# First keys through two DMA queues, in halves of 64 partitions, and one load for the last heads' rows

## The chip, the cores and the metric

The kernel runs on one core of one Trainium2 chip. The core has a matrix engine (TensorE, PE in the profile), a vector engine (VectorE, DVE), a scalar engine (ScalarE, ACT), GpSimd (POOL) and SyncE (SP), which here only issues transfers. Transfers are issued from SP's queue and from ACT's queue. The metric is device time in microseconds: 193.44 us is the median of 3 runs before (193.33 to 193.98). The profiled execution took 193.34 us, and its span, on which all times below are counted, is 191.2 us.

## What is computed

One token is decoded with 32 heads over the last 4096 positions of a key and value cache, and the result is gated by a small multilayer network on the same input:

```python
xn = _layernorm(x)
q = (xn @ wq).reshape(1, 1, 32, 128)           # one query row for each head
k = k_cache[:, :, Sk - 4096:, :]               # 32 heads x 4096 x 128, bf16
v = v_cache[:, :, Sk - 4096:, :]
p = softmax((q @ k^T) * 128 ** -0.5)
s = (p @ v) @ wo                               # 4096 -> 512
g = silu(B(xn, w1, w2, w3, w4))                # layernorm, gelu, w3, gelu, w4
out = x + s * g
```

(The lines are shortened; B is the network.) With a sequence of one position every part of B's first layer is shifted out, so w1 has no effect on the output and the kernel doesn't load it. The keys and values are 32 MB each, 79 MB are moved in all, and each byte is used once.

## The kernel before

**Tiling.** The heads are handled in eight groups of four (G = 4). A group's keys are one tile `kv` of 128 partitions by 128 columns by 128 numbers in bf16, 4 MB; partition 4b + a holds block b of head a. `load_kv` (L95) loads such a tile as 128 rows, whole (32 KB a row) or cut along the columns. Group 0's keys come as two loads, columns 0 to 63 and 64 to 127 (L534), so that each has all 128 partitions.

**Scores.** Two engines share a group. VectorE takes the first 64 or 80 columns: `k_vector` (L312) multiplies a quarter of them with the query (product, L321) and sums it (L323), four pairs a group. TensorE takes the other columns: `k_turn` transposes them (L339), ScalarE copies the result out of PSUM (L342), and `k_scores` (L350) multiplies with the query. ScalarE separates the heads (`sm_own`, L359), VectorE adds them to the scores and finds the maximum (`sm_max`, L364, L366), and `sm_turn`, `sm_exp`, `sm_den` and `sm_rden` make the softmax a step later.

**Values and output.** `v_wide` (L427) multiplies a group's probabilities with its values, `v_turn`, `v_add` and `v_out` turn and scale the result. `ox_spread`, `ox_pick` and `y_wide` multiply heads 0 to 27 with wo. The last group's values come in three loads (columns 0 to 63, 64 to 95, 96 to 127). The last 32 columns go through `v_part` (L461), and the last four heads through `y_head`, which reads the tile `wo_rows`, loaded by `load_rows` (L414) as two loads of two heads.

**Order.** The loop at L531 runs ten steps. In step s the keys of group s are scored, and the values of group s - 2 are used. Inside the region opened at L527 the order of TensorE, VectorE and ScalarE is the order in which the code is written.

**Queues and buffers.** `load` (L75) issues every large load on SP, in program order: w2, w3, w4 (1280 KB), the remaining 96 rows of w4, the keys of groups 0, 1 and 2, and so on. ACT issues x twice and wq (4 MB). An issue that has to wait, for a free buffer or for an earlier landing, holds up those behind it on its queue. There are three key buffers: group 3's keys can be loaded only when VectorE and TensorE have finished with group 0's. There are two value buffers. The weights `wts` are freed before the first values are loaded, so that load waits for the last reader of the weights (the copy `hr`, L273, and the product after it).

Of the kernel before, what the change touches and what calls it, by code (L numbers as in the profile page):

```python
# [8 lines left out]
P = 128  # L9
BF16 = mybir.dt.bfloat16  # L10
# [8 lines left out]
G = 4  # L19
# [7 lines left out]
def kernel(  # L27
# [14 lines left out]
    nc = tc.nc  # L42
# [3 lines left out]
    _, H, Sk, Dh = A_k_cache.shape  # L46
# [3 lines left out]
    W0 = Sk - W  # L50
    assert W == 4096
    CP = G * W // P
    PB = P // G
# [6 lines left out]
    k_pool = ctx.enter_context(tc.tile_pool(name="k", bufs=K_BUFS))  # L60
# [11 lines left out]
    wts_guard = tc.tile_pool(name="wts", bufs=1)  # L72
    wts = wts_guard.__enter__()

    def load(dst, src):  # L75
        return tc.keep_in_program_order(nc.sync.dma_start(out=dst, in_=src))  # L76

    x_bf = small.tile([P, KC], BF16, name="x_bf")
    nc.scalar.dma_start(out=x_bf[:], in_=A_x.rearrange("a b (p c) -> p (a b c)", p=P))
# [3 lines left out]
    wq_sb = wts.tile([P, KC, HD], BF16, name="wq_sb")  # L83
    nc.scalar.dma_start(out=wq_sb[:].rearrange("p c n -> p (c n)"),
                        in_=A_wq.rearrange("(a b c) n -> b a (c n)", a=4, c=KC))
    w2_sb = wts.tile([P, KC, D], BF16, name="w2_sb")
    load(w2_sb[:], B_w2.rearrange("(p c) n -> p c n", p=P))
    w3_sb = wts.tile([P, KC, F], BF16, name="w3_sb")
# [1 line left out]
    w4_sb = wts.tile([P, 11, D], BF16, name="w4_sb")  # L90
    load(w4_sb[:, 0:10, :], B_w4[0:10 * P, :].rearrange("(p c) n -> p c n", p=P))
    load(w4_sb[0:96, 10, :], B_w4[10 * P:F, :])


    def load_kv(pool, cache, g, cuts=(0, CP)):  # L95
        t = pool.tile([P, CP, Dh], BF16, tag="kv", name="kv")
        src = cache[0, G * g:G * g + G, W0:, :].rearrange("a (b c) d -> b a (c d)", b=PB)
        dst = t[:].rearrange("p c d -> p (c d)")
        for c0, c1 in zip(cuts, cuts[1:]):
            load(dst[:, c0 * Dh:c1 * Dh], src[:, :, c0 * Dh:c1 * Dh])  # L100
        return t
# [115 lines left out]
    for b in range(2):  # L217
# [5 lines left out]
        for t in range(2):  # L223
            rows = slice(64 * t, 64 * t + 64)
            nc.scalar.copy(out=q_pair[rows, 4 * b:4 * b + 4, :, G * t:G * t + G].rearrange("p g l a -> p g a l"),
                           in_=qt_ps[rows].bitcast(BF16).rearrange("p g (a m l) -> p g a m l", a=G, l=2)[:, :, :, 0, :])
# [41 lines left out]
    for i, (col, w) in enumerate(terms):  # L268
        r = 32 * (i % 4)
# [41 lines left out]
    def k_open(g):  # L311
        st[g] = {  # L312
            "sT": ps_s.tile([P, CP - 64, G], FP32, tag="sT", name="sT"),
            "S": sm_pool.tile([P, CP], FP32, tag="S", name="S"),
        }

    def k_vector(g, kn, part):
        m = nd(g) // 4
        rows = slice(m * part, m * part + m)
        prod = prod_pool.tile([P, 20, Dh], BF16, tag="prod", name="prod")  # L320
        nc.vector.tensor_tensor(out=prod[:, 0:m, :], in0=kn[:, rows, :],  # L321
                                in1=q_bc[:, g:g + 1, :].to_broadcast([P, m, Dh]), op=ALU.mult)
        nc.vector.tensor_reduce(out=st[g]["S"][:, rows], in_=prod[:, 0:m, :], axis=AX.X, op=ALU.add)  # L323
# [3 lines left out]
    def batches(g):  # L327
        n, m = nd(g), CP - nd(g)
        k = -(-m // 8)
        edges = [n + 2 * (m // 2 * i // k) for i in range(k + 1)]  # L330
        return list(zip(edges, edges[1:]))

    def k_turn(g, kn, b):
        c0, c1 = batches(g)[b]
        n = (c1 - c0) // 2
        pt = ps_tr.tile([P, 4, P], FP32, tag="pt", name="pt")
        for i in range(n):
            c = c0 + 2 * i
            nc.tensor.transpose(pt[:, i, :], kn[:, c:c + 2, :].rearrange("p c d -> p (c d)").bitcast(FP32),  # L339
                                ident_f[:])  # L340
        kts[b] = kt_pool.tile([P, 4, 2 * P], BF16, tag="kt", name="kt")
        nc.scalar.copy(out=kts[b][:, 0:n, :], in_=pt[:, 0:n, :].bitcast(BF16))  # L342

    def k_scores(g, b):
        kt = kts.pop(b)
        c0, c1 = batches(g)[b]
        for i in range((c1 - c0) // 2):
            c = c0 + 2 * i - nd(g)
            for l in range(2):
                nc.tensor.matmul(st[g]["sT"][:, c:c + 2, :].rearrange("p c a -> p (c a)"),  # L350
                                 lhsT=kt[:, i, l::2], rhs=q_pair[:, g, l, :], start=(l == 0), stop=(l == 1))
# [44 lines left out]
    def sm_rden(g):  # L396
        s = st[g]
        s["rden"] = sm_pool.tile([P, G], FP32, tag="rden", name="rden")
        nc.vector.reciprocal(out=s["rden"][:], in_=s["den"][:])  # L399
# [7 lines left out]
    def load_wo(i):  # L407
        h0, n = blocks[i]
        load(wo_blk[i], A_wo[h0 * P:(h0 + n) * P, :].rearrange("(p t) n -> p t n", p=P))
# [4 lines left out]
    def load_rows(h, n):  # L414
        load(wo_rows[:, h - h_part:h - h_part + n, :],
             A_wo[h * P:(h + n) * P, :].rearrange("(h p) n -> p h n", p=P))
# [108 lines left out]
    NG = H // G  # L525
# [5 lines left out]
    for s in range(NG + LAG):  # L531
        h = s - LAG
        last = h == NG - 1
        kn = load_kv(k_pool, A_k_cache, s, (0, 64, CP) if s == 0 else (0, CP)) if s < NG else None  # L534
        if s == LAG:
            wts_guard.__exit__(None, None, None)
            v_pool = ctx.enter_context(tc.tile_pool(name="v", bufs=V_BUFS))
            wo_blk[2] = v_pool.tile([P, 4, D], BF16, tag="wo_4", bufs=1, name="wo_4")
            wo_rows = v_pool.tile([P, H - h_part, D], BF16, tag="wo_rows", bufs=1, name="wo_rows")
        if last:  # L540
            v = load_kv(v_pool, A_v_cache, h, cuts)
            for r in (H - G, H - 2):
                load_rows(r, 2)
        elif h >= 0:
            v = load_kv(v_pool, A_v_cache, h)
        if h == 3:
            wo_24 = k_pool.tile([P, 32, D], BF16, tag="kv", name="wo_24")
            wo_blk[0], wo_blk[1] = wo_24[:, 0:16, :], wo_24[:, 16:24, :]
            load_wo(0)
        if h == 5:  # L550
            load_wo(1)
            load_wo(2)

        if s < NG:
            nb = len(batches(s))

            def keys(b0, b1):
                for b in range(b0, b1):
                    k_turn(s, kn, b)
                    if b > 0:  # L560
                        k_scores(s, b - 1)

            k_open(s)
            k_vector(s, kn, 0)
            keys(0, 2)
            if s == 7:
                v_turn(h - 1)
                v_add(h - 1)
                v_out(h - 1)
            elif s > 1:  # L570
                sm_den(s - 2)
                sm_rden(s - 2)
            elif s == 1:
                sm_max(0)
            k_vector(s, kn, 1)
            keys(2, 4)
            if s == 7:
                sm_den(h)
                sm_rden(h)
                keys(4, nb - 2)  # L580
                sm_turn(s - 1)
                keys(nb - 2, nb)
            else:
                if s > 0:
                    sm_turn(s - 1)
                keys(4, nb)
            k_scores(s, nb - 1)
            sm_own(s)
            if s == 7:
                k_vector(s, kn, 2)  # L590
                v_wide(h, v)
                sm_exp(s - 1)
                v_turn(h)
                y_open()
                k_vector(s, kn, 3)
                v_add(h)
                v_out(h)
                ox_spread(1)
                sm_max(s)
                continue  # L600
            if s > 0:
                sm_exp(s - 1)
            if h > 0:
                v_turn(h - 1)
            k_vector(s, kn, 2)
            if h >= 0:
                v_wide(h, v)
            if h > 0:
                v_add(h - 1)
                v_out(h - 1)  # L610
            if s == 6:
                ox_spread(0)
            k_vector(s, kn, 3)
            if s == 6:
                ox_pick(0)
            if s > 0:
                sm_max(s)
        elif s == NG:
            ox_pick(1)
            sm_turn(NG - 1)  # L620
            sm_exp(NG - 1)
            y_wide(1, False)
            sm_den(NG - 2)
            sm_rden(NG - 2)
            y_wide(0, False)
            warm(3)
            v_wide(h, v)
            sm_den(NG - 1)
            sm_rden(NG - 1)
            v_turn(h)  # L630
            v_add(h)
            v_out(h)
            ox_spread(2)
        else:
            v_open(h)
            warm(3)
            v_wide(h, v, cuts[1], last=False)
            ox_pick(2)
            y_wide(2, True)
            nc.scalar.copy(out=y_sum[:], in_=yr[0][:].rearrange("p j n -> p (j n)"))  # L640
            v_wide(h, v, cuts[2], cuts[1])
            v_turn(h)
            v_add(h)
            rows_add(y_ps, ind, y_sum, False)
            v_part(h, v, cuts[2], CP)
            v_out(h)
            for r in range(H - G, H):
                y_head(r)
# [36 lines left out]
```

## Time and profile before

| What | Value |
|---|---|
| median time | 193.44 us |
| span of the profiled execution | 191.2 us |
| VectorE busy | 150.9 us (79%) |
| TensorE busy | 116.4 us (61%) |
| ScalarE busy | 89.2 us (47%) |
| moved by DMA | 79.02 MB, 413 GB/s over the span |
| wq landed | 17.6 us after its issue at 2.32 us |
| group 0's second half landed | 27.4 us after its issue at 4.71 us |
| group 1 of VectorE starts | 41.91 us |

How to read the profile: the second part of the page cuts the span into 40 slices of 4.8 us, and each digit is the busy share of an engine in tenths, 9 for 90% or more. A timeline line gives the start, the busy time, the engine, the line of the kernel, the operation with output and input, and in brackets how long the engine had been idle before it and what ended the wait. A line on a DMA issue gives the tile, the queue, the number of issues, the size of one and the median time from issue to landing. Buffer numbers are left out of names, so that w_sb is w2, w3 or w4.

### The profile page before, as it was taken

How to read it: one execution, taken by the hardware profiler on the slowest of the kernel's cores; microseconds unless marked ns; L12 is line 12 of the kernel's file. 1: busy time of each engine (PE TensorE's matmuls, PEld its weight loads, DVE VectorE, ACT ScalarE, POOL GpSimd, SP SyncE). 2: the span in 40 equal slices, each digit the busy share in tenths (PEclk: the TensorE clock that was granted, in tenths of full speed). 3: DMA queues.
4: the chain of work that ended last, by engine and by line, in shares of the span. 5: the costliest groups of instructions: out<-in, count | busy, mean ns of one | idle time of the engine just before them, and what ended most of it. 6: DMA issues, size and time to landing. Idle time of an engine off the chain costs nothing.

```text
span 191.2 us, 2839 instructions
## 1 busy us (share of the span) xinstructions
PE 116.4 (61%) x1159; PEld 74.2 (39%) x1159; DVE 150.9 (79%) x175; ACT 89.2 (47%) x191; POOL 2.3 (1%) x11
## 2 busy tenths in 40 slices
PE   1653754989825368256845772680888189739762
PEld 0430222767614334143334441540763077313322
DVE  1660159979999999999999999999999999980111
ACT  2001370888794076427464564542475148733120
POOL 2110000000000000000000000000000000000000
PEclk9999695555755557955695588557567858975998
DMA  6999999999999999999999999999999998999990
GB/s 211 447 430 404 431 418 439 439 439 437 432 434 439 432 429 432 432 439 432 422 432 432 418 422 418 452 439 435 439 432 434 435 432 372 471 425 405 420 371 32
DMA packets 4572, 79.02 MB, mean 413 GB/s; under 512 B 624, under 2 KB 1232, under 8 KB 1488
## 3 DMA queue, kind: packets, MB, share of 16 engines
q1 hardware_dynamic: 4264, 74.65, 91.6%
q10 hardware_dynamic: 296, 4.20, 5.1%
q8 instruction: 9, 0.15, 0.3%
q14 instruction: 3, 0.02, 0.0%
HBM read 78.84 MB, written 0.00 MB: 412 GB/s over the span
## 4 chain that ended last, share of the span: by engine, by line
DVE 46%; DMA 43%; PE 5%; ACT 3%; issue 1%; SPq 1%; ACTq 0%; DVEq 0%
DMA kv<-in_A_k_cache_dram 31%; DVE S L323 28%; DVE prod L321 15%; DMA kv<-in_A_v_cache_dram 10%; ACT kt L342 3%; DMA x_bf<-in_A_x_dram 2%; PE pt L339 2%; PE ov L427 1%; DVE m L366 1%; DVE S L364 1%; SPq L76 1%; PE sT L350 1%; DVE mx L374 1%; PE oT L461 1%; PE ot_ps L444 0%
## 5 line engine op out<-in xcount | busy, mean ns | idle before, releaser
L323 DVE TENSOR_REDUCE S<-prod 128x20 f32<-128x2560 bf16 (+1 forms) x32 | 86.0, 2686 | 1.1
L342 ACT COPY kt<-pt 128x1024 bf16<-128x1024 bf16 x52 | 51.2, 1013 | 40.4 <-PE pt L339 38.7
L339 PE MATMUL pt<-ident_f,kv 128*128 128x128 f32 x208 | 46.7, 376 | 10.8 <-DMA kv<-in_A_k_cache_dram 10.8
L321 DVE TENSOR_TENSOR prod<-kv,q_bc 128x2560 bf16<-128x2560 bf16 (+1 forms) x32 | 45.4, 1418 | 3.9 <-DMA kv<-in_A_k_cache_dram 3.7
L339 PEld LDWEIGHTS pt<-ident_f,kv 128*128 128x128 f32 x208 | 34.2, 196 | 14.4 <-DMA kv<-in_A_k_cache_dram 10.5
L350 PE MATMUL sT<-q_pair,kt 128*128 128x8 bf16 x416 | 19.4, 170 | 15.7 <-ACT kt L342 15.5
L350 PEld LDWEIGHTS <-kt 128*128 128x128 bf16 x416 | 16.4, 104 | 26.8 <-ACT kt L342 25.8
L427 PE MATMUL ov<-kv,pT 128*16 128x512 bf16 x248 | 22.0, 515 | 1.4 <-DMA kv<-in_A_v_cache_dram 1.4
L388 ACT ACTIVATE pT<-S,mb 128x128 bf16<-128x128 f32 x32 | 13.9, 573 | 0.3
L372 PE MATMUL mt_ps<-ident_f,m 128*1 128x128 f32 x8 | 2.9, 359 | 17.4 <-DVE rden L399 16.9
L433 ACT COPY ov_sb<-ov 128x512 f32<-128x512 f32 x8 | 4.7, 586 | 17.1 <-PE ov L427 17.1
L427 PEld LDWEIGHTS <-pT 128*16 128x16 bf16 x248 | 6.9, 109 | 13.2 <-issue 11.4
L359 ACT ACTIVATE own<-sT,par 128x48 f32<-128x48 f32 (+1 forms) x32 | 7.5, 356 | 3.7 <-PE sT L350 3.7
L444 PE MATMUL ot_ps<-ident_f,ov_sb 128*128 128x128 f32 x32 | 7.1, 359 | 2.9 <-ACT mb L384 1.9
L211 DVE CAST q_row<-qr_ps 128x512 bf16<-128x512 f32 x1 | 0.7, 692 | 9.9 <-PE qr_ps L208 9.9
L388 ACT ACTIVATION_READ_ACCUMULATOR pT<-S,mb 128x1 f32 x32 | 8.3, 258 | 0.0
L372 PEld LDWEIGHTS mt_ps<-ident_f,m 128*1 128x1 f32 x8 | 0.6, 80 | 17.9 <-DVE rden L399 17.2
L399 DVE RECIPROCAL rden<-den_ps 128x4 f32<-128x4 f32 x8 | 1.4, 175 | 7.0 <-PE den_ps L394 7.0
L381 PE MATMUL mb_ps<-md,par_t 5*128 5x4 f32 x16 | 3.9, 311 | 4.1 <-DVE md L376 4.1
L255 ACT ACTIVATE a_row<-a_ps 128x384 bf16<-128x384 f32 x1 | 0.5, 491 | 12.0 <-remote 12.0
L444 PEld LDWEIGHTS ot_ps<-ident_f,ov_sb 128*128 128x128 f32 x32 | 4.5, 178 | 3.9 <-ACT mb L384 2.3
L208 PE MATMUL qr_ps<-wq_sb,xq_bf 128*1 128x512 bf16 x32 | 3.1, 566 | 3.7 <-DMA wq_sb<-in_A_wq_dram 3.7
(122 smaller groups left out, 81.6 us busy)
## 6 DMA issues: line engine op xcount, KB each, us to landing
kv<-in_A_k_cache_dram SPq DMA_DIRECT2D x7, 4096.0 KB, 31.3
kv<-in_A_v_cache_dram SPq DMA_DIRECT2D x7, 4096.0 KB, 30.6
wq_sb<-in_A_wq_dram ACTq DMA_DIRECT2D x1, 4096.0 KB, 17.6
kv<-in_A_k_cache_dram SPq DMA_DIRECT2D x2, 2048.0 KB, 27.4
wo<-in_A_wo_dram SPq DMA_DIRECT2D x1, 2048.0 KB
kv<-in_A_v_cache_dram SPq DMA_DIRECT2D x1, 2048.0 KB
kv<-in_A_v_cache_dram SPq DMA_DIRECT2D x2, 1024.0 KB, 17.6
w_sb<-in_B_w_dram SPq DMA_DIRECT2D x1, 1376.0 KB, 9.1
```

What stands on the lines that cost most here:

```text
L321: nc.vector.tensor_tensor(out=prod[:, 0:m, :], in0=kn[:, rows, :], in1=q_bc[:, g:g + 1, :].to_broadcast([P, m, Dh]), op=ALU.mult)
L323: nc.vector.tensor_reduce(out=st[g]["S"][:, rows], in_=prod[:, 0:m, :], axis=AX.X, op=ALU.add)
L339: nc.tensor.transpose(pt[:, i, :], kn[:, c:c + 2, :].rearrange("p c d -> p (c d)").bitcast(FP32), ident_f[:])
L342: nc.scalar.copy(out=kts[b][:, 0:n, :], in_=pt[:, 0:n, :].bitcast(BF16))
L350: nc.tensor.matmul(st[g]["sT"][:, c:c + 2, :].rearrange("p c a -> p (c a)"), lhsT=kt[:, i, l::2], rhs=q_pair[:, g, l, :], start=(l == 0), ...
L359: nc.scalar.mul(s["own"][:, 0:m, a], s["sT"][:, 0:m, a], par[:, a:a + 1])
L372: nc.tensor.transpose(mt_ps[:], s["m1"][:], ident_f[:])
L381: nc.tensor.matmul(mb_ps[:], lhsT=par_t[:].rearrange("k b a -> k (b a)"), rhs=md[:], start=True, stop=True)
L388: nc.scalar.activation(out=s["pT"][:, :, a], in_=s["S"][:], func=ACT.Exp, scale=scale, bias=mb[:, a:a + 1], accum_out=s["sum"][:, a:a + 1])
L427: nc.tensor.matmul(ov[r:r + 4 * G], lhsT=s["pT"][:, c:c + 4, :].rearrange("p i a -> p (i a)"), rhs=v[:, c:c + 4, :], start=(i < 4), stop=( ...
L433: nc.scalar.copy(out=s["ov_sb"][:], in_=ov[:])
L444: nc.tensor.transpose(ot_ps[:, step * j:step * j + P], s["ov_sb"][:, j, :], ident_f[:])
```

## The change

The keys of groups 0, 1 and 2 are now loaded ahead of the loop by `keys_load`, and split between two queues. Groups 0 and 1 come as two loads each: partitions 0 to 63 on SP, behind the weights, and partitions 64 to 127 on ACT, behind wq. Group 2 comes as one load on ACT. It is meant to let the first keys travel on two queues side by side. Group 0 is no longer cut along its columns. At the end, the rows of wo for the last four heads are one load of 512 KB where there were two of 256 KB.

```diff
-    def load(dst, src):
-        return tc.keep_in_program_order(nc.sync.dma_start(out=dst, in_=src))
+    def load(dst, src, engine=None):
+        return tc.keep_in_program_order((engine or nc.sync).dma_start(out=dst, in_=src))
...
+    kvs = {}
+
+    def keys_load(g, b0, b1, engine):
+        if g not in kvs:
+            kvs[g] = k_pool.tile([P, CP, Dh], BF16, tag="kv", name="kv")
+        load(kvs[g][G * b0:G * b1].rearrange("p c d -> p (c d)"),
+             A_k_cache[0, G * g:G * g + G, W0:, :].rearrange("a (b c) d -> b a (c d)", b=PB)[b0:b1], engine)
...
+    keys_load(0, 0, PB // 2, nc.sync)
+    keys_load(0, PB // 2, PB, nc.scalar)
+    keys_load(1, 0, PB // 2, nc.sync)
+    keys_load(1, PB // 2, PB, nc.scalar)
+    keys_load(2, 0, PB, nc.scalar)
...
-        kn = load_kv(k_pool, A_k_cache, s, (0, 64, CP) if s == 0 else (0, CP)) if s < NG else None
+        kn = kvs[s] if s in kvs else load_kv(k_pool, A_k_cache, s) if s < NG else None
...
-            for r in (H - G, H - 2):
-                load_rows(r, 2)
+            load_rows(H - G, G)
```

## The prediction

> **What bounds the kernel now.** I read the page's slices first. The DMA row stands at full load from 5 us to the end, and VectorE's row from the seventh slice to the thirty-sixth:
>
> ```profile
> DVE  1660159979999999999999999999999999980111
> ...
> DMA  6999999999999999999999999999999998999990
> GB/s 211 447 430 404 431 418 439 439 439 437 432 434 439 432 429 432 432 439 432 422 432 432 418 422 418 452 439 435 439 432 434 435 432 372 471 425 405 420 371 32
> ```
>
> So two resources are full at once. The transfers need 79 MB at some 430 GB/s, about 184 us; VectorE works through eight groups one after another. Which sets the end? For that I took VectorE's timeline at the start, where its chain begins:
>
> ```profile
> 26.09 1.23 DVE L321 TENSOR_TENSOR prod<-kv,q_bc 128x2048 bf16<-128x2048 bf16 x1 [2.19 <-DMA kv<-in_A_k_cache_dram]
> ...
> 33.79 1.23 DVE L321 TENSOR_TENSOR prod<-kv,q_bc 128x2048 bf16<-128x2048 bf16 x1
> ...
> 37.37 1.22 DVE L321 TENSOR_TENSOR prod<-kv,q_bc 128x2048 bf16<-128x2048 bf16 x1
> ...
> 41.91 1.49 DVE L321 TENSOR_TENSOR prod<-kv,q_bc 128x2560 bf16<-128x2560 bf16 x1 [0.99 <-DMA kv<-in_A_k_cache_dram]
> ```
>
> It starts when the first half of group 0's keys has landed. One pair of product and sum takes 37.37 - 33.79 = 3.58 us, four make a group: 14.3 us. Group 1 starts at 41.91, and from there VectorE's waits for keys add up to 0.5 us. The timeline of the tail shows how near that chain is to the end:
>
> ```profile
> 170.29 0.29 DVE L366 TENSOR_REDUCE m<-S 128x1 f32<-128x128 f32 x1
> ...
> 170.77 0.37 PE L372 MATMUL mt_ps<-ident_f,m 128*1 128x128 f32 x1 [0.54 <-DVE pick L492]
> ...
> 181.50 1.04 PE L427 MATMUL ov<-kv,pT 128*16 128x512 bf16 x16 [1.02 <-DMA kv<-in_A_v_cache_dram]
> ...
> 183.93 0.61 PE L427 MATMUL ov<-kv,pT 128*16 128x512 bf16 x8 [0.41 <-DMA kv<-in_A_v_cache_dram]
> ...
> 186.38 0.96 PE L461 MATMUL oT<-pT,kv 128*128 128x4 bf16 x32 [0.17 <-DMA kv<-in_A_v_cache_dram]
> ```
>
> After the last maximum (170.3) TensorE and ScalarE work nearly without a pause until the last values; they wait for DMA only 1.02 + 0.41 + 0.17 = **1.6 us**. So the end belongs to the transfers, and VectorE's chain has 1.6 us of slack behind it: a start of group 0 that is later by more moves the end.
>
> [...]
>
> ```profile
> wq_sb<-in_A_wq_dram ACTq DMA_DIRECT2D x1, 4096.0 KB, 17.6
> ...
> w_sb<-in_B_w_dram SPq DMA_DIRECT2D x1, 1280.0 KB, 19.2
> ...
> w_sb<-in_B_w_dram SPq DMA_DIRECT2D x1, 96.0 KB, 19.1
> ```
>
> wq (ACT, from 2.3 us) has rows of 32 KB, w4 (SP) rows of 10 KB, and the smaller load lands after the larger: one row for one row, not byte for byte. The trace's records of single packets show it directly: from 10.7 us on each engine takes a 10 KB row in 0.385 us and a 32 KB row in 1.213 us in turn, and a semaphore write of 4 bytes uses up a turn too. [...] The trace agrees for w4's last 96 rows (six small rows on each of 16 engines); so 64 rows will be four on each of 16. [...]
>
> **The change, part by part.**
>
> *Group 0 in two halves of partitions.* VectorE reads all 128 partitions, so it now waits for both halves, 4 MB, where it waited for columns 0 to 63 of all partitions, 2 MB. The question is when the later half lands. The ACT half stands right behind wq; the SP half behind w2, w3, w4 and the 96-row rest of w4. Per engine, in packet turns: wq's eighth row ends at 18.6. SP then still holds three rows of w4, six 1 KB rows and two semaphore writes, and gives one per turn; ACT gives a 32 KB row per turn, first four of group 0, then four of group 1. Those 8 turns cost 8 x 1.213 = 9.7 us, w4's three rows 1.16, the rest 0.3: 29.8. Only then does the SP half of group 0 begin, and now each of its four rows alternates with a row of group 2 (ACT): 8 x 1.213 = 9.7, so 39.5, and 1.3 from the last row to the landing (as wq: 18.6 to 19.9): **40.8**, against 26.09 for the first half and about 32.1 for the second (issued at 4.7, 27.4 to landing). The halves do not run side by side; the tiny rows cost the SP ring its turns.
>
> *The ports.* [...] the eight ACT rows go to 64 partitions while SP sends almost nothing: twice the time, +9.7 us. The four SP rows, each beside a full-width row of group 2, lose between 0 and 4.85; I take 2.4, and the same for group 1's SP half. Then group 0 lands at 40.8 + 9.7 + 2.4 = **52.9**. Without a port limit both terms are 0.
>
> *What VectorE does then.* Its four pairs start at 52.9 and end at 67.2 (hr and bv, 0.9 us, lay inside them before; I take it that they go ahead of the keys now; if not, +0.9). Group 1 lands at 39.5 + 9.7 + 1.3 + 9.7 + 4.85 = 65.0, no wait. So group 1 starts 67.2 - 41.91 = 25.3 us later. Of this, 0.5 (its wait for group 6) and 0.4 (its wait for a maximum at 161.5) come back, and the tail's slack of 1.6: +22.8 us. The transfers end later too, by 9.7 + 4.85 and by gaps where a key or value buffer comes free late, but the last values, at about 186.4 + 14.6 and a few us, stay ahead of a tail at 186.4 + 22.8.
>
> *ACT's queue.* Three issues of about 0.6 us each. The SP queue waited for earlier landings before some issues (for x_bf 1.4 us, x_row 0.9, wq 12.5); the third one on ACT would likely wait for wq, to 19.9. Queued behind it are the GELU of L255 (16.2 before) and the q copies (21.8 before): 0 to 1 us later, and hidden, since the keys land at 40.8 at the earliest. SP saves its issues of the same size, off every path.
>
> *w4's rest lands later* (31 or 40 instead of 21): hr and with it the first value load come later by 5 to 15 us, hidden by keys in flight until 49 or later.
>
> *Last heads' rows as one load.* One issue of 0.5 us less, the same 1 KB rows, the same landing near 187. Nothing, since VectorE's o at 187.37 comes before their use.
>
> **Rivals.** (A) *Turns, but no port limit*: landing 40.8, group 0 done at 55.1, shift 13.2 - 0.9 - 1.6 = +10.7: 204.1. For it: the packets of before show 27 GB/s per engine and nothing of a port[...]. (B) *Both halves really travel side by side and land with 12 MB moved, near 32.1*: four pairs to 46.4, shift 4.5 - 0.5 - 1.6, about +2.4: 195.8. It needs the ring with tiny rows not to lose its turns; the landing of w4 after wq speaks against it. (C) *Not slower*: the halves gain what VectorE waits for today (2.19 + 0.99 + 0.5, less what the tail allows), or a second ring keeps the engines fuller; at best 193.44 - 1.5 = 192. Against it: the DMA share is already 1.00 to 1.04 over 20 to 180 us, and no order brings all of group 0 before 11.6 MB have moved. (D) *Ports at their worst*, both SP halves doubled as well: group 0 at 55.4, group 1 at 69.9, shift 28.0 - 0.9 - 1.6 = +25.5: 218.9.
>
> **How the numbers follow.** The port case with its bounds (my forecast and D, 213 to 219): 0.54. A: 0.30. B: 0.07. C or no change: 0.09. The likeliest is 193.44 + 22.8 = 216.2. The range goes from A less 1 us to D plus 1: 203 to 220, and leaves out B and C. Chances: slower by over 0.3% is 0.54 + 0.30 + 0.07 = 0.91, within it 0.03, faster 0.06.
>
> **What would show it.** VectorE's first product: at 26 (C), 32 (B), 41 (A), 50 to 55 (ports). The landings: ACT's halves well before SP's. DMA GB/s between 20 and 40 us: about 220 with the port limit, 430 without. VectorE without waits after that, the tail's three waits for values gone, and the last maximum later by the same shift as group 1. It is wrong if the halves land together, if the engines keep turns by bytes, if ACT's issues come so late that SP's small rows pass alone, or if TensorE's clock, 0.5 at 170 to 176 us, is so different in the tail that more than 1.6 us comes back.

## The result and the profile after

The changed kernel takes **225.16 us** (224.55 to 225.76, 5 runs) where the kernel before takes 193.44: the ratio is 1.1633, with a 95% interval from 1.1598 to 1.1667. That is 31.7 us slower. The forecast was slower by 22.8 us, with a range up to 220: the direction was right, the size too small. The span of the profiled execution is 222.9 us (191.2 before).

The slices of the page after, 5.6 us each:

```profile
DVE  1730100000979699999999999999999999894011
...
DMA  7999999999999999999999999889999999968940
GB/s 237 436 451 335 256 197 194 282 259 306 282 279 276 394 440 442 406 459 415 435 447 406 450 394 438 353 323 435 470 391 453 407 438 416 431 294 279 406 165 3
```

VectorE stands still in slices 6 to 10. In these slices the DMA row still shows 9: the engines are as busy as before, but they move 194 to 306 GB/s instead of 430. A full DMA row alone doesn't show that transfers go at full rate; the row under it does. The last two columns of the next lines are the DMA share and the mean in GB/s. Two stretches before:

```profile
20.00:40.00 20.00, 14.41 (x136) 8.73 (x134) 14.51 (x12) 11.00 (x17) 0.00 (x0) 0.67 1.04 443
40.00:72.00 32.00, 19.66 (x200) 15.21 (x202) 30.59 (x24) 21.48 (x45) 0.00 (x0) 0.55 1.00 428
```

The same two after:

```profile
20.00:40.00 20.00, 5.30 (x45) 1.97 (x41) 0.69 (x1) 6.80 (x12) 0.00 (x0) 0.67 0.97 210
40.00:72.00 32.00, 11.41 (x121) 7.16 (x121) 14.58 (x11) 10.37 (x14) 0.00 (x0) 0.61 0.99 278
```

In the first, ACT's halves (partitions 64 to 127) are on the engines nearly alone (in the trace the first 32 KB row on SP starts at 39.4); in the second, SP's halves (partitions 0 to 63) in turn with group 2's rows, which go to all 128. The issues after, with the median time to landing:

```profile
kv<-in_A_k_cache_dram SPq DMA_DIRECT2D x2, 2048.0 KB, 69.7
kv<-in_A_k_cache_dram ACTq DMA_DIRECT2D x2, 2048.0 KB, 26.4
kv<-in_A_k_cache_dram ACTq DMA_DIRECT2D x1, 4096.0 KB, 54.3
...
w_sb<-in_B_w_dram SPq DMA_DIRECT2D x1, 96.0 KB, 39.1
```

Of each pair of halves the profile has one landing only: group 0's half on ACT landed 26.4 us after its issue at 4.78, so at 31.2, and group 1's half on SP at 74.3. Group 0's half on SP is seen in VectorE, which waits for it until 56.12. The two halves of group 0 land 25 us apart, and 96 KB of w4, which landed after 19.1 us before, now take 39.1. VectorE's timeline after shows what that costs:

```profile
56.12 1.23 DVE L335 TENSOR_TENSOR prod<-kv,q_bc 128x2048 bf16<-128x2048 bf16 x1 [32.16 <-DMA kv<-in_A_k_cache_dram]
...
63.16 0.68 DVE L287 COPY hr<-hr_ps 128x512 f32<-128x512 f32 x1
...
66.14 0.29 DVE L292 TENSOR_TENSOR bv<-xn_row,h_ps 128x128 f32<-128x128 f32 x1 [1.17 <-PE h_ps L169]
...
74.42 1.49 DVE L335 TENSOR_TENSOR prod<-kv,q_bc 128x2560 bf16<-128x2560 bf16 x1 [2.22 <-DMA kv<-in_A_k_cache_dram]
```

(`hr` and `bv` are two small steps of the network B.) Group 0 starts at 56.12 instead of 26.09, group 1 at 74.42 instead of 41.91, 32.5 us later. From there to the end nothing gets shorter by much: the tail after has no wait for values any more.

```profile
203.13 0.29 DVE L380 TENSOR_REDUCE m<-S 128x1 f32<-128x128 f32 x1
...
213.96 1.04 PE L441 MATMUL ov<-kv,pT 128*16 128x512 bf16 x16
...
215.81 0.60 PE L441 MATMUL ov<-kv,pT 128*16 128x512 bf16 x8
...
218.14 0.94 PE L475 MATMUL oT<-pT,kv 128*128 128x4 bf16 x32
```

None of the three products with values has a bracket (they waited 1.02, 0.41 and 0.17 us before): the values are there when TensorE comes. The last maximum lies 203.13 - 170.29 = 32.8 us later, the end 31.7.

### The profile page after: what moved, and what is told of

It reads as the page before. It is cut to its first block, busy times and chain, and to the rows that moved or that the text cites. A ratio compares the mean times of both kernels' runs of the same rounds, so it can differ in the third digit from the quotient of the medians.

```text
span 222.9 us, 2841 instructions
## 1 busy us (share of the span) xinstructions
PE 119.4 (54%) x1159; PEld 73.9 (33%) x1159; DVE 151.0 (68%) x175; ACT 90.3 (40%) x192; POOL 2.3 (1%) x11
## 3 DMA queue, kind: packets, MB, share of 16 engines
q10 hardware_dynamic: 600, 12.59, 19.1%
## 4 chain that ended last, share of the span: by engine, by line
DVE 59%; another core or an unknown queue 15%; PE 13%; DMA 8%; ACT 2%; issue 1%; ACTq 0%; POOL 0%; DVEq 0%; POOLq 0%
DVE S L337 35%; DVE prod L335 18%; DMA wq_sb<-in_A_wq_dram 8%; PE ov L441 3%; PE pt L353 2%; PE qr_ps L222 1%; PE yr_ps L532 1%; DVE S L378 1%; DVE m L380 1%; PE wm L521 1%; ACT kt L356 1%; PE ot_ps L458 1%; PE hr_ps L284 1%; DVE mx L388 1%
## 5 line engine op out<-in xcount | busy, mean ns | idle before, releaser
L356 ACT COPY kt<-pt 128x1024 bf16<-128x1024 bf16 x52 | 51.1, 1012 | 72.2 <-PE pt L353 70.6
L353 PE MATMUL pt<-ident_f,kv 128*128 128x128 f32 x208 | 45.3, 366 | 31.4 <-DMA kv<-in_A_k_cache_dram 27.8
L353 PEld LDWEIGHTS pt<-ident_f,kv 128*128 128x128 f32 x208 | 33.2, 190 | 35.5 <-issue 35.5
L364 PEld LDWEIGHTS <-kt 128*128 128x128 bf16 x416 | 16.5, 104 | 28.0 <-ACT kt L356 26.7
L441 PE MATMUL ov<-kv,pT 128*16 128x512 bf16 x248 | 24.4, 561 | 0.0
L224 ACT ACT_TABLE_LOAD x1 | 1.3, 1283 | 20.5 <-DMA wq_sb<-in_A_wq_dram 20.5
L395 PEld LDWEIGHTS mb_ps<-md,par_t 5*128 5x128 f32 x16 | 3.7, 289 | 7.2 <-PE sT L364 4.6
## 6 DMA issues: line engine op xcount, KB each, us to landing
kv<-in_A_k_cache_dram ACTq DMA_DIRECT2D x2, 2048.0 KB, 26.4
```

The costliest lines, as they stand in the source:

```text
L395: nc.tensor.matmul(mb_ps[:], lhsT=par_t[:].rearrange("k b a -> k (b a)"), rhs=md[:], start=True, stop=True)
L441: nc.tensor.matmul(ov[r:r + 4 * G], lhsT=s["pT"][:, c:c + 4, :].rearrange("p i a -> p (i a)"), rhs=v[:, c:c + 4, :], start=(i < 4), stop=( ...
```

## The experiments

Two theories stood against each other. **Half rate and turns** (the forecast's): a load to the lower or the upper 64 partitions goes at half rate, and each small row of SP gives ACT the turn of a long row. The first is what the prediction and the expectations call ports, port limit, port loss or port theory. No trace shows a port, and the factor of two was assumed: every large load of before covers 128 partitions. **Queues**: two queues side by side, ACT's queue, or 64-row loads are slow as such.

**Halves in the middle of the run.** Group 5's keys alone, on SP, far from the small rows and from ACT's loads:

```diff
...
+        for b0, b1 in ((0, PB // 2), (PB // 2, PB)):
+            load(t[G * b0:G * b1].rearrange("p c d -> p (c d)"), src[b0:b1])
...
```

> The kernel before, with the keys of group 5 alone (in the middle of the run, one queue, no small rows near) as two loads of 64 partitions, 0 to 63 and 64 to 127. Port theory: these 4 MB move at half rate, 19.4 us instead of 9.7; the transfers set the end, so 193.4 + 9.7 = 203.1 us, and the packets' rate over the stretch falls to about 215 GB/s. Rival (the halves were slow because of the two queues, of ACT's queue or of the small rows): 193.4 us.

It took 204.34 us, ratio 1.0562 (1.0545 to 1.0579): +10.9, where the half rate had 9.7. The stretch in which group 5 moves, in the kernel before:

```profile
96.00:118.00 22.00, 13.26 (x147) 8.85 (x145) 21.73 (x19) 12.59 (x27) 0.00 (x0) 0.77 1.00 428
```

And with the halves:

```profile
96.00:118.00 22.00, 10.07 (x105) 6.41 (x105) 19.27 (x17) 8.98 (x23) 0.00 (x0) 0.69 1.04 236
```

The DMA share is 1.04 and the rate 236 GB/s. The trace also has a record of each packet, with its size and its time; here a packet is one row, and a row of 32 KB takes 2.5 us instead of 1.21. One queue, no small rows: the halves by themselves go at half rate.

> The control of the run before: group 5's keys as two loads of all 128 partitions, 64 columns each. Port theory: 193.4 us[...]. Rival (two loads instead of one, or shorter rows, cost the time): slower, as much as with halves of partitions.

Cut along the columns: 193.32 us, ratio 0.9992 (0.9982 to 1.0001). Two loads instead of one, and rows of half the length, cost nothing.

The third of this set keeps 64 rows of 32 KB but puts them on every second partition:

```diff
...
+        for a in range(2):
+            load(t[a:P:2].rearrange("p c d -> p (c d)"),
+                 A_k_cache[0, G * g + a:G * g + G:2, W0:, :].rearrange("a (b c) d -> b a (c d)", b=PB))
...
```

> Group 5's keys as two loads of 64 rows again, but to the even and to the odd partitions. [...] If the number of rows (64, four on an engine) is what halves the rate: 203.1 us, as for the partition halves. If the ports do: less. [...] My guess is between, 196 to 200 us.

193.23 us, ratio 0.9998 (0.9987 to 1.0008). My guess of 196 to 200, between no loss (193.4) and the half rate (203.1), was wrong: nothing at all is lost. The same stretch:

```profile
96.00:118.00 22.00, 13.74 (x139) 9.14 (x138) 21.73 (x19) 12.29 (x27) 0.00 (x0) 0.66 0.99 427
```

So neither the number of rows nor their size halves the rate (236 and 427 GB/s at the same 64 rows of 32 KB), but which 64 rows go together. What slows the ones that do is not shown. Nor is it settled whether the partitions matter: since partition 4b + a holds block b of head a, the cut also changes what is read together, half of the blocks of all four heads or all blocks of two heads. No run varies the one without the other. Which row an engine takes was not seen, and why even and odd rows lose nothing stays open.

**The last heads' rows alone.** Only `load_rows(H - G, G)` in the kernel before.

> The kernel before with only the last four heads' rows of wo as one load. Every theory: no change, 193.4 us (within 0.5): the rows are used at 187.6 us on the span, and one load of the same bytes lands near 187. If the first two heads' rows now landed too late, up to +0.6 us.

193.5 us, ratio 1.0001 (0.9991 to 1.0011). This part of the change is nothing.

**Group 0 uncut.** The kernel before with `(0, CP)` for every group's keys.

> The kernel before, with group 0's keys as one load of all 128 partitions and columns, on SP as before. This is the first ingredient of the change alone: VectorE waits for 4 MB instead of 2. No port limit, no turns: first product near 32 us (the second half landed there before), group 1 of VectorE at 46.5 to 48 instead of 41.9, of which 0.8 to 1.6 comes back: 197 to 199 us. If VectorE's start didn't matter to the end (transfers alone set it): 193.4.

197.59 us, ratio 1.0207 (1.0179 to 1.0234). Its timeline on VectorE:

```profile
32.29 1.23 DVE L321 TENSOR_TENSOR prod<-kv,q_bc 128x2048 bf16<-128x2048 bf16 x1 [3.67 <-DMA kv<-in_A_k_cache_dram]
...
46.61 1.49 DVE L321 TENSOR_TENSOR prod<-kv,q_bc 128x2560 bf16<-128x2560 bf16 x1
```

To wait for 4 MB instead of 2 costs 6.2 us at the start, 4.7 at group 1 and some 4 at the end, without any second queue. Nothing else changed, so VectorE's start does reach the end.

**The turns without the half rate.** The changed kernel with even and odd partitions for the halves of groups 0 and 1:

```diff
...
-        load(kvs[g][G * b0:G * b1].rearrange("p c d -> p (c d)"),
-             A_k_cache[0, G * g:G * g + G, W0:, :].rearrange("a (b c) d -> b a (c d)", b=PB)[b0:b1], engine)
+        load(kvs[g][a:P:2].rearrange("p c d -> p (c d)"),
+             A_k_cache[0, G * g + a:G * g + G:2, W0:, :].rearrange("a (b c) d -> b a (c d)", b=PB), engine)
...
```

(Group 2's load stays whole and on ACT; it is written out apart.)

> The changed kernel with the halves of groups 0 and 1 to the even partitions (SP) and the odd partitions (ACT): same queues, same order, same number and size of rows[...]. Theory: the port loss is gone (430 GB/s over 20 to 72 us), the turns stay: group 0's SP half still waits for some eight turns of 1.21 us, lands near 41, group 1 of VectorE at 57 to 58 instead of 42, time 207 to 209 us. Rival (64-row halves on two queues are slow however they lie): 225.

209.34 us, ratio 1.0813 (1.0782 to 1.0843). The rate over 20 to 40 us and VectorE's first product:

```profile
20.00:40.00 20.00, 5.55 (x45) 2.00 (x44) 0.69 (x1) 6.80 (x12) 0.00 (x0) 0.67 1.01 434
```

```profile
41.49 1.22 DVE L337 TENSOR_TENSOR prod<-kv,q_bc 128x2048 bf16<-128x2048 bf16 x1 [17.29 <-DMA kv<-in_A_k_cache_dram]
...
58.35 1.49 DVE L337 TENSOR_TENSOR prod<-kv,q_bc 128x2560 bf16<-128x2560 bf16 x1
```

434 GB/s on the same two queues, with the same order and the same number and size of rows: the theory of slow queues falls. The first product at 41.49 is close to the forecast's landing without the half rate (40.8). This kernel is 15.8 us faster than the changed one: that much is the part of the half rate, by whatever it comes about. The changed kernel with all keys on one queue (below) is as much slower than group 0 uncut: 213.44 - 197.59 = 15.9.

**The small rows first.** One line of the even and odd kernel moved, the 96 KB rest of w4 from last weight to first load:

```diff
+    load(w4_sb[0:96, 10, :], B_w4[10 * P:F, :])
     load(w2_sb[:], B_w2.rearrange("(p c) n -> p c n", p=P))
...
-    load(w4_sb[0:96, 10, :], B_w4[10 * P:F, :])
```

> Even and odd partitions, and the 96-row rest of w4 as the first load on SP: no port loss, and three lost turns instead of nine or ten. First product at 34 to 35 us, group 1 at 50 to 51, time 200 to 202 us, and steady from run to run. If it stays near 208, the turns of the small rows were not the cause.

202.63 us, ratio 1.0468 (1.0445 to 1.0490); first product at 35.66, group 1 at 51.79, each a little above what was expected. A load of 96 KB, moved forward, is worth 209.34 - 202.63 = 6.7 us.

**Halves of columns.** `keys_load` with columns 0 to 63 on SP and 64 to 127 on ACT, and then also with the rest of w4 first:

> The changed kernel with the halves of groups 0 and 1 cut along the columns (64 columns on all 128 partitions, rows of 16 KB), same queues and same order. Theory (ports and turns): no half rate, so 430 GB/s over 20 to 40 us; what is left is the turns: the SP half of group 0 still waits for some eight turns of 0.61 us and then alternates with 16 KB rows, landing near 36 us; first product at 36, group 1 of VectorE at about 51 instead of 42; 202 us (199 to 205). Rival (the two queues or ACT's queue themselves are slow): 216 us or more, with the rate still near 210 GB/s.

204.21 us, ratio 1.0540 (1.0496 to 1.0585); 431 GB/s over 20 to 40 us; first product at 37.41, group 1 at 54.06. That is some 2 us above the expected middle: hr and bv stand between VectorE's first pairs, bv waited 1.70 us, and group 0 took 16.7 us instead of 14.3.

> Both repairs: halves of columns, and the 96-row rest of w4 first. What remains is that SP and ACT share the engines, so that the SP half of group 0 lands with nearly all of the ACT half: first product near 33 us, 199 us. It stays slower than before (193.4), since before no byte of the second half stood ahead of the first. If turns of small rows don't matter, the same time as with halves of columns alone.

200.76 us, ratio 1.0378 (1.0352 to 1.0404); first product at 34.47, group 1 at 50.59; 199 and 33 were expected. Again the small rows: 3.5 us, about half of the 6.7 above, which fits rows of 16 KB instead of 32 in ACT's halves.

**The small rows first, in the changed kernel itself.**

> The changed kernel with one line moved: the 96-row rest of w4 (96 KB, 1 KB rows) is the first load on SP instead of the last weight. Turn theory: SP loses only three turns after wq, not nine or ten, and the halves of group 0 really travel side by side: first product at 36 to 47 us instead of 56, time 207 to 218 instead of 225. If the small rows don't matter: 225, first product at 56.

The four runs lie between 211.90 and 220.17 us. The profiled one took 217.40; VectorE's first product came at 48.07, above the expected 36 to 47, and group 1 at 65.72. Its stretches:

```profile
20.00:40.00 20.00, 7.15 (x45) 2.85 (x44) 0.69 (x1) 5.52 (x11) 0.00 (x0) 0.50 1.02 225
40.00:56.00 16.00, 7.31 (x57) 4.31 (x58) 7.86 (x7) 3.21 (x4) 0.00 (x0) 0.50 0.92 201
```

Now both halves are in flight together, which is what the change was for, and the rate is still half. In the packet records the rows of both queues take about 2.4 us. The engines are not all on the same half, either: at 41.0 us eleven of the sixteen carry a row of SP's half and five a row of ACT's, and every one of these rows takes 2.33 us. By estimate, five engines at full rate would move 5 x 27 = 135 GB/s (32 KB in 1.21 us is 27 GB/s), less than the 203 to 236 that one half took alone. So a limit that all engines on a half share would not slow these five, and what each row is held back by stays open. The two halves at once gain nothing to speak of: 201 to 225 GB/s, against 203 to 236 for one alone. As the times of this kernel spread widely, I take from it no size, only that it stays far above 193.

**All keys on one queue.** The changed kernel with `nc.sync` in all five loads.

> The changed kernel with all five loads of keys on SP, halves of partitions as in the change. Theory: no turns are lost, but the halves come one after the other at half rate: group 0 lands at 20.1 + 19.4 + 1.3 = 40.8, group 1 at 60.2, group 1 of VectorE starts 18.3 later than before, of which some 0.8 comes back: 211 us. Rival (turns alone, no half rate): group 0 lands at 31.4 and the time is about 198.

213.44 us, ratio 1.1031 (1.1008 to 1.1055); 203 GB/s over 40 to 56 us; first product at 42.05, group 1 at 60.95, after a wait of 4.62 us for keys. No turns are lost, the half rate remains: 2.4 us above what was expected.

**Group 2 on SP.** The disputed term of the forecast: what a row of group 2 costs in turn with an SP half.

```diff
-    keys_load(2, 0, PB, nc.scalar)
+    keys_load(2, 0, PB, nc.sync)
```

> The changed kernel with group 2's keys on SP, behind group 1's half, instead of on ACT. ACT's halves come as before (to about 40 us), then the SP halves are alone on the engines, at half rate but without a row of group 2 in turn with each: four rows of 2.4 us, group 0 lands at about 51 instead of 56, group 1 at about 61 instead of 74, group 1 of VectorE at 67 instead of 74.4: 217 to 218 us. If sharing with group 2's rows cost nothing: 225.

218.95 us, ratio 1.1323 (1.1276 to 1.1370). VectorE's timeline:

```profile
51.64 1.23 DVE L335 TENSOR_TENSOR prod<-kv,q_bc 128x2048 bf16<-128x2048 bf16 x1 [27.18 <-DMA kv<-in_A_k_cache_dram]
...
67.77 1.49 DVE L335 TENSOR_TENSOR prod<-kv,q_bc 128x2560 bf16<-128x2560 bf16 x1
```

Group 0 lands 4.5 us earlier than in the changed kernel and group 1 needs no wait: 6.2 us of the time came from group 2 on ACT. In the packet records the rows of SP's halves, now alone, take 2.55 us.

The kernels whose start was moved, but for the one whose runs spread, in one table, in us. The starts are those of one profiled run, the time is the median, and the time of the profiled run differs from it by up to 0.7 us:

| Kernel | first product | group 1 starts | time | time less group 1 |
|---|---|---|---|---|
| before | 26.09 | 41.91 | 193.44 | 151.5 |
| group 0 uncut | 32.29 | 46.61 | 197.59 | 151.0 |
| columns, small rows first | 34.47 | 50.59 | 200.76 | 150.2 |
| even and odd, small rows first | 35.66 | 51.79 | 202.63 | 150.8 |
| columns | 37.41 | 54.06 | 204.21 | 150.2 |
| even and odd | 41.49 | 58.35 | 209.34 | 151.0 |
| one queue | 42.05 | 60.95 | 213.44 | 152.5 |
| group 2 on SP | 51.64 | 67.77 | 218.95 | 151.2 |
| changed | 56.12 | 74.42 | 225.16 | 150.7 |

The last column hardly moves: over a range of 32 us the time is the start of VectorE's group 1 plus 150 to 152.5. None of the versions beats the kernel before.

## Why the prediction was right and where it was wrong

**What bounds the kernel**: right. Transfers set the end before, VectorE's chain stood just behind it, and a later start goes through to the end (group 0 uncut, and the table).

**The turns**: right in mechanism and, for the landing, in size. Without the half rate the forecast had it at 40.8; the even and odd kernel's first product is at 41.49. The small rows' turns are shown by moving one load (6.7 us), and in the packet records of the changed kernel the 96 small rows come in bursts some 2.5 us apart, from 26.7 to 37.9 us, with ACT's 32 KB rows of 2.5 us between them. The time that rival A drew from this, 204.1, was still 5.2 short of that kernel's 209.34, and rival B's 195.8 was 1.8 short of group 0 uncut: what comes back later and, for A, hr and bv (both below) were mis-sized there too.

**The half rate**: right in effect and size (2.5 us for ACT's rows against 1.21), but assumed; its cause is not shown. ACT's eight rows were to take 9.7 us more and end near 39.2; in the packet records the last of them ends between 39.4 and 40.4 on the sixteen engines.

**The step that failed** is the term "The four SP rows, each beside a full-width row of group 2, lose between 0 and 4.85; I take 2.4, and the same for group 1's SP half". It charged the SP rows alone; group 2's rows were left at 1.21 us, at no loss and without a reason. In the packet records both lose: over 40 to 70 us SP's rows take 2.1 us, and group 2's beside them 1.75. (Half of group 2's rows go to the same 64 partitions; that this is why they lose is not shown.) Four of each take some 15.4 us, where 9.7 + 2.4 = 12.1 was reckoned, and even the stated bound of 14.6 is passed. So group 0 landed at 56.1 instead of 52.9. Group 2 on SP, where no such turns are, gave 51.64.

Group 1 landed at 74.3 instead of 65.0, for three reasons. The rows of both SP halves took longer, some 5 us in all. Between the halves SP's turn went to a semaphore write, and a whole row of group 2, 1.2 us, ran beside it. And one engine came last: fifteen of the sixteen had ended SP's rows by 70.55 us, the last at 73.15. As far as start and end times tell, it is the engine that took 1.39 us at 62.50 for a packet of 16 KB of another queue ("q8 instruction" on the page) and fell behind its neighbours by a row. The load landed at 74.34, 1.2 us after its last engine was done.

So the wait for group 1, which the forecast excluded, came back. Group 1 started at 74.4 instead of 67.2, **+7.2 us**: 3.2 for the later landing, 1.8 as group 0 took 16.1 us instead of 14.3 (hr and bv, below), 2.2 of wait. Without the late engine the keys would have landed some 2.6 us earlier (an estimate from the two ends), just before VectorE was done with group 0 at 72.2.

**The second term that was off** is what comes back later: 0.5 + 0.4 + 1.6 = 2.5 us reckoned, 32.5 - 31.7 = 0.8 measured, **+1.7 us**. From group 1 to the last maximum it took 128.7 us after and 128.4 before: the wait for group 6 went, but VectorE waited 0.7 for a product of TensorE (at L464) instead. From the last maximum to the end 1.1 of the 1.6 us came back. By the table, the other kernels returned 0.3 to 1.4 us, but for one queue, which lost another 1.0. Why so little came back was not pursued. Together 22.8 + 7.2 + 1.7 = 31.7.

**hr and bv** were taken to go ahead of the keys; in the changed kernel they stayed between VectorE's first pairs and bv waited 1.17 us, so that group 0 took 16.1 us instead of 14.3. It cost nothing here, as the wait for group 1 (2.22 us) would have been longer by as much. In the kernels without that wait it counts: in the even and odd kernel group 0 took 16.9 us. It is so in all seven kernels with keys on ACT's queue. Group 0 uncut and one queue have none there; in both hr and bv were done before the keys came, and group 0 took 14.3. So some 2.5 us of the even and odd kernel's loss are neither half rate nor turns.

**ACT's queue**: the wait was right, its price not. ACT's third issue waited for wq and freed ACT at 20.5. The q copies came 0 to 3 us later, but the GELU, put behind them in ACT's order, came at 27.4 instead of 16.2, 11 us later. With group 2 on SP, where ACT's issues were done at 7.0, it still came at 27.9, so the order put it there and not the wait for wq. The first value load came 35 us later (66.18 instead of 31.19), not 5 to 15. In the changed kernel the wait for the keys covers both. **The last rows**: right, no change.

**The range** ended too early at the top. Its upper end was not a bound: it let the SP halves double, but kept group 2's rows at 1.21 us.

**Two readings** were slightly off, with no weight: the DMA share over 20 to 180 us is 0.99 to 1.04, and the loads up to group 0 add up to 11.7 MB, not 11.6.

## What to carry to other kernels

Cut a load along the columns or by every second partition, not into the lower and the upper 64 partitions (427 against 236 GB/s here), and look at GB/s and not at the DMA share, which shows busy engines at half rate too. Before a load is put on a second queue, count the rows that stand ahead of it on either queue: in these kernels each small row of one queue gave the other a turn of a long row, and 96 KB of them moved forward were worth 6.7 us. When a resource is full and the next chain stands 1.6 us behind it, a forecast has to charge both sides of every pair of loads that travel together (here 2.1 and 1.75 us a row, where 1.21 was reckoned for the second), or its upper end is none.

## What was not expected of the hardware

64 rows on every second partition go at full rate (427 GB/s, 32 KB rows at 1.21 us) on one queue and on two (434). The halves lost slightly more than a factor of two: 2.5 us for a row against 1.21, and +10.9 us for 4 MB where 9.7 were reckoned. Two halves in flight together on two queues gave 201 to 225 GB/s, no more than one alone (203 to 236), and the five engines on the one half were as slow as the eleven on the other.
